# A new order for a projection's seven products, earlier regroups, later deviations, and another queue for the filters, in an FFT-filter and SoLU kernel

The kernel runs on 1 core of one Trainium2 chip. The metric is the device time of one execution in microseconds (us), lower is better. Times are medians; a ratio is the mean time of one kernel's fast runs over the mean of the kernel before's fast runs of the same rounds, so it is not quite the ratio of the two medians.

## The reference

A Fourier filter over the sequence, then an expansion with a softmax-weighted activation and a layer norm, all in fp32 (in short form, not the file's own lines):

```python
X = np.fft.rfft(x, axis=1)                      # x: 8 x 3136 x 256
y = np.fft.irfft(X * (filt_r + 1j * filt_i), n=3136, axis=1)
h = y.reshape(25088, 256) @ w_in                # 256 -> 1024
e = np.exp(h - h.max(-1, keepdims=True))
solu = h * e / (e.sum(-1, keepdims=True) + 1e-9)
ln = (solu - solu.mean(-1)) / np.sqrt(solu.var(-1) + 1e-6) * g_ln
out = ln @ w_out                                # 1024 -> 256
```

## The kernel before

The Fourier part is done as matmuls (pa, pb, the filter multiplication on VectorE, pc, py), entry by entry, beside the expansion of the entries already done. Its last pc matmul starts at 1368 us in this kernel; some py matmuls follow until 1547 us. What comes after is called the pure part: only the two layers are left, and the last four pairs, with no first layer beside them, are the tail.

Tokens are taken in 98 pairs of blocks of 128. Both layers of a pair are done by seven products each (a Strassen-Winograd scheme), which share few banks of PSUM, the memory that TensorE's sums stand in (m0 to m2 for the first layer, o0 and o1 for the second): a product either starts a bank or adds to what stands in it, and between two of them ScalarE or VectorE must take the intermediate sum away. This is called an evacuation, or a hand-over where TensorE waits for it. Here are the second layer's products, called P1 to P7 below; the first layer's are called by number alone.

```python
def project(p, m):
    bank = {1: 0, 6: 0, 5: 0, 3: 0, 2: 1, 7: 1, 4: 1}[m]
    if m in (1, 2):
        pos[p, bank] = ps_o.tile(...)           # one buffer for o0, one for o1
    s1, s2, s3, s4 = solu_sums[p]               # sums of regrouped rows, from GpSimd
    lhs = {1: solu_ts[p, 0][0], 2: solu_ts[p, 0][1], 4: solu_ts[p, 1][1], 5: s1, 6: s2, 7: s3, 3: s4}[m]
    for f in range(KF // 2):
        nc.tensor.matmul(out=pos[p, bank], lhsT=lhs[:, f, :], rhs=w[:, f, :],
                         start=f == 0 and m in (1, 2, 7), ...)
```

The program order is written by hand, one step per block, two steps per pair. The order of the products, with the bar standing for the work on the other engines in the middle of a step:

| | even step | odd step |
|---|---|---|
| before | 1, P5, 2 / 6, P3, P4, 7 | 5 / P1, P2, 3, 4, P6, P7 |
| after | 1, P6, 2 / P5, 6, 7, P3 | P1, P2, 5 / P7, 3, 4, P4 |

Two kinds of transfer matter here, both through SyncE's queue. `regroup` turns the activated rows into the layout that the projection reads, with eight DMAs of 128 KB per pair; it reads the result of the turn, a transposition on VectorE. `regroup_deviations` does it for the layer norm's factors (`rs_t`), with four DMAs of 0.5 KB per two pairs. Every evacuation of a projection multiplies by `rs_t`, so the first one of a pair cannot start without it. The code, cut at the dots:

```python
# even step, before                    # odd step, before
...                                    ...
regroup(j - 3, 0)  # 4 DMAs, then      project_sums(j - 3, 0)
                   # rows <- rs        if (j - 3) % 2 == 0:
...                                        regroup_deviations((j - 3) // 2)   # a pair ahead of use
project(p, 3); project(p, 4)           project(p, 6); project(p, 7)
regroup(j - 3, 1)  # 4 DMAs
```

Of the kernel before, what the change touches and what calls it, by code (L numbers as in the profile page):

```python
# [80 lines left out]
def kernel(  # L81
# [70 lines left out]
    class Spectrum:  # L152
# [72 lines left out]
        def multiply(self, i, parts):  # L225
# [14 lines left out]
            if 1 in parts:  # L240
                turned, pt = self.turned.pop(i), self.prods[i]
                nc.vector.tensor_tensor(out=turned, in0=turned, in1=part(1), op=ALU.mult)  # L242
                nc.vector.tensor_tensor(out=pt, in0=pt, in1=turned, op=ALU.add)
                del self.fs[i]
# [38 lines left out]
    with ExitStack() as st:  # L283
# [93 lines left out]
        for i in range(NS):  # L377
            sp.turn(i)
            sp.multiply(i, (0, 1))
# [40 lines left out]
    def load_filter(s, count):  # L420
        f = fpool.tile([P, 2, 2, C], FP32, name=f"f_{s}", tag="f")
        for p in range(2):
            nc.gpsimd.dma_start(out=f[NQ * p:NQ * p + NQ, 0:count],
                                in_=f_dram[s:s + count].rearrange("s q k c -> q s k c"))
        return f
# [135 lines left out]
    def regroup(p, i):  # L561
# [10 lines left out]
        if not second and i == 0:  # L572
# [4 lines left out]
            rs_rows[g] = rows = rs_dram.tile([P, 4], FP32, name=f"rows_{g}", tag="rows")  # L577
            nc.sync.dma_start(out=rows, in_=rs)
# [23 lines left out]
    def project(p, m):  # L602

        bank = {1: 0, 6: 0, 5: 0, 3: 0, 2: 1, 7: 1, 4: 1}[m]
# [17 lines left out]
    def keep_out(p, i, to):  # L622
        rs = out_half(p, i, 0)[1]
        nc.scalar.activation(out=out_half(p, *to)[0], in_=pos[p, 0], func=AFT.Copy, scale=rs)  # L624

    def finish_out(p, i, n, kept, bank):
        ot, rs = out_half(p, i, n)
        if kept is None:
            nc.vector.tensor_scalar(out=ot, in0=pos[p, bank], scalar1=rs, scalar2=None, op0=ALU.mult)  # L629
        else:  # L630
            nc.vector.scalar_tensor_tensor(out=ot, in0=pos[p, bank], scalar=rs,  # L631
                                           in1=out_half(p, *kept)[0], op0=ALU.mult, op1=ALU.add)

    def store_out(p):
# [13 lines left out]
        [[] for _ in range(blocks + LAG + 1)] for _ in range(8))  # L648
# [17 lines left out]
    for n in range(1, len(GROUPS)):  # L666
# [11 lines left out]
        for i, t in enumerate(spread(len(sp.units), *spectrum_at)):  # L678
# [5 lines left out]
            for part in range(2):  # L684
# [24 lines left out]
    def step(k):  # L709
        j, odd = divmod(k, 2)  # L710
        p = j - (LAG - 1) // 2 if odd else j - (LAG + 1) // 2
        if not 0 <= p < pairs:
            p = None
        hid, proj = k < blocks, p is not None
        if odd and j + 1 < pairs:
            pair_sums(j + 1)
        for job in stores[k] + products[0][k] + first_of[k]:
            job()
        if not odd:
# [3 lines left out]
            if proj:  # L723
                project(p, 5)
                keep_out(p, 1, (0, 1))
            if hid:
                product(j, 2)
        else:
            if hid:
                product(j, 5)  # L730
                keep(j, k - 1, 1)
# [4 lines left out]
        for job in products[1][k]:  # L736
            job()
        if not odd:
            if proj:
                finish_out(p, 1, 1, (0, 1), 1)  # L740
            if hid:
                finish(j, k, 0, (k, 0), 1)
        elif hid:
            finish(j, k, 1, (k - 1, 1), 2)
        if 2 <= k < blocks + 2:
            exponential(k - 2)
        for job in early[k]:
            job()
        if not odd:
            if hid:  # L750
                product(j, 6)
                keep(j, k + 1, 0)
            if proj:
                project(p, 3)
                project(p, 4)
            if 0 <= j - 3 < pairs:
                regroup(j - 3, 1)
            if 0 <= j - 4 < pairs:
                project_sums(j - 4, 1)
            if hid:  # L760
                product(j, 7)
        else:
            if proj:
                project(p, 1)
                keep_out(p, 0, (0, 0))
                project(p, 2)
                finish_out(p, 0, 0, (0, 0), 1)
# [3 lines left out]
            if 0 <= j - 3 < pairs:  # L771
                project_sums(j - 3, 0)
                if (j - 3) % 2 == 0:
                    regroup_deviations((j - 3) // 2)
            if proj:
                project(p, 6)
                project(p, 7)
        if 2 <= k < blocks + 2:
            normalize(k - 2)
        if not odd:  # L780
            if proj:
                finish_out(p, 0, 1, None, 0)
                finish_out(p, 1, 0, (1, 0), 1)
                store_out(p)
        else:
            if hid:
                finish(j, k - 1, 1, None, 0)
                finish(j, k, 0, (k, 0), 2)
            if proj:
                keep_out(p, 1, (1, 0))  # L790
# [39 lines left out]
```

## Time and profile before

| | before |
|---|---|
| median | 1791.24 us (3 runs, 1781.95 to 1801.8); 1786.6 us in the rounds with the changed kernel |
| span of the profiled run, granted clock | 1779.0 us, 0.979 |
| TensorE's bare work (see below) | 1611.8 us |
| gaps between matmuls | 161.3 us: 115 up to 400 us, 33 from 400 to 1700 us, 13 after |

The two last rows are reckoned as the prediction does it: each matmul record is given the distance at which such records follow each other when nothing waits (0.429, 0.216 and 0.112 us for 512, 256 and 128 columns), and whatever the next start lies later is a gap. Busy times can't be used for that, as the ends of pipelined matmuls are modelled. The lines themselves are shown in the prediction.

In profile lines PE is TensorE (PEld its weight loads), DVE VectorE, ACT ScalarE, POOL GpSimd, and SPq SyncE's queue. The lines of kernel.py that matter, before and (in brackets) changed: first layer's products L500 (L502), projection's L612 (L619), filter product pb L210; ScalarE's scaling by `rs_t` L624 (L631), VectorE's L629 (L636) and L631 (L638); the first layer's reductions L521 and L524 (L523 and L526), the normalization between them L548 (L550).

### The profile page before, as it was taken

The page shows a single profiled execution, that of the slowest core. Times are in us where ns is not written, and L with a number is a line of the kernel's source. Part 1 is how long each engine was busy: PE and PEld are TensorE (multiplying, and loading weights), DVE is VectorE, ACT ScalarE, POOL GpSimd, SP SyncE. Part 2 cuts the span into 40 slices and gives each one's busy share as a digit, 9 for nine tenths or more (in the row PEclk, how much of TensorE's full clock was granted, in tenths as well). Part 3 has the DMA queues.
Part 4 walks back from the last instruction along what each step waited for, and adds up shares of the span by engine and source line. Part 5 has one row for each costly group of instructions (what it writes and reads, how often), then busy time and mean ns, then how long its engine had stood idle before and what let it go on. Part 6 is the DMA issues. An engine that isn't in the chain of part 4 may idle for free.

```text
span 1779.0 us, 28627 instructions
## 1 busy us (share of the span) xinstructions
PE 1671.6 (94%) x8692; PEld 1141.3 (64%) x8692; DVE 1244.1 (70%) x2586; ACT 1068.4 (60%) x1917; POOL 1093.9 (61%) x1290
## 2 busy tenths in 40 slices
PE   6688887899999999999999999989999999999996
PEld 1225445676666666766667667767777777777776
DVE  0793654578877875678798766767767777777773
ACT  2365555566767666666667666656666566655551
POOL 3242354677767775667877656546666656676664
PEclk9789998999999999999999999999999999999999
DMA  9876687897788865566777665557776444444443
GB/s 279 259 253 184 207 216 197 245 247 211 201 240 231 223 173 158 135 188 188 195 188 200 156 153 157 139 141 186 192 188 158 113 116 114 120 106 107 104 114 94
DMA packets 358120, 314.57 MB, mean 177 GB/s; under 512 B 60833, under 2 KB 318882, under 8 KB 357968
## 3 DMA queue, kind: packets, MB, share of 16 engines
q1 hardware_dynamic: 295664, 187.23, 41.0%
q0 software_dynamic: 29152, 86.45, 16.3%
q10 hardware_dynamic: 33152, 39.07, 7.7%
q8 instruction: 71, 1.16, 0.3%
q14 instruction: 81, 0.66, 0.1%
HBM read 131.65 MB, written 81.50 MB: 120 GB/s over the span
## 4 chain that ended last, share of the span: by engine, by line
PE 74%; DMA 11%; DVE 6%; ACT 3%; issue 3%; SPq 1%; POOL 1%; ACTq 0%; POOLq 0%; DVEq 0%
PE o L612 28%; PE m L500 28%; PE py L277 6%; PE pa L183 4%; PE pb L210 4%; PE pc L252 3%; DMA t<-d 2%; DMA x<-in_x_dram 2%; DMA d<-t 2%; DVE h L548 1%; DMA solu_t<-turn 1%; DMA f<-f_dram 1%; DMA de<-de_tbl 1%; ACT e L532 1%; DVE i L242 1%
## 5 line engine op out<-in xcount | busy, mean ns | idle before, releaser
L550 ACT ACTIVATE e<-h,nmu 128x1024 f32<-128x1024 f32 x196 | 225.3, 1150 | 307.9 <-DVE h L548 305.7
L612 PE MATMUL o<-w_out_sb,solu_t 128*128 128x128 f32 x3136 | 401.9, 277 | 3.0 <-DVE ot L629 1.9
L612 PEld LDWEIGHTS o<-w_out_sb,solu_t 128*128 128x128 f32 x3136 | 382.1, 193 | 33.6 <-issue 28.5
L500 PE MATMUL m<-w_in_sb,s 128*128 128x512 f32 x784 | 397.3, 598 | 6.3 <-ACT h L510 6.3
L612 PEld LDWEIGHTS o<-w_out_sb,u 128*128 128x128 f32 x2352 | 306.5, 192 | 148.7 <-issue 115.7
L612 PE MATMUL o<-w_out_sb,u 128*128 128x128 f32 x2352 | 312.7, 276 | 9.0 <-ACT ot L624 7.7
L479 POOL TENSOR_TENSOR u<-solu_t 128x512 f32<-128x512 f32 x98 | 153.9, 1571 | 265.8 <-DMA solu_t<-turn 152.3
L500 PE MATMUL m<-w_in_sb,y 128*128 128x512 f32 x588 | 304.5, 601 | 6.3 <-DVE h L521 3.5
L548 DVE SCALAR_TENSOR_TENSOR h<-e,rsum,h 128x1024 f32<-128x1024 f32 x196 | 291.8, 1489 | 7.1 <-DVE rsum L545 0.3
L631 DVE SCALAR_TENSOR_TENSOR ot<-o,rs_t,ot 128x128 f32<-128x128 f32 x294 | 102.5, 349 | 257.3 <-ACT ot L624 216.6
L479 POOL TENSOR_TENSOR u<-solu_t,u 128x512 f32<-128x512 f32 x98 | 144.7, 1477 | 173.1 <-PE o L612 171.6
L558 DVE STREAM_TRANSPOSE turn<-h 128x1024 f32<-128x1024 f32 x196 | 242.2, 1236 | 1.5
L524 DVE CUSTOM_DVE_ANT_0 h<-m,h 128x512 f32<-128x512 f32 x196 | 134.8, 688 | 138.3 <-ACT h L510 89.8
L510 ACT COPY h<-m 128x512 f32<-128x512 f32 x294 | 173.0, 589 | 91.3 <-PE m L500 77.9
L532 ACT ACTIVATE e<-h,nmax 128x1024 f32<-128x1024 f32 x196 | 224.5, 1146 | 0.0
L500 PEld LDWEIGHTS m<-w_in_sb,s 128*128 128x128 f32 x784 | 130.6, 192 | 79.2 <-issue 74.2
L277 PEld LDWEIGHTS py<-wi_t,t 100*128 100x128 f32 x1024 | 133.3, 195 | 62.9 <-issue 39.8
L183 PE MATMUL pa<-x,wf_t 98*100 98x512 f32 x256 | 141.7, 662 | 26.6 <-DMA x<-in_x_dram 20.7
L479 POOL TENSOR_TENSOR solu_t<-solu_t,solu_t 128x512 f32<-128x512 f32 x98 | 157.0, 1602 | 7.7
L277 PE MATMUL py<-wi_t,t 100*128 100x98 f32 x1024 | 134.9, 277 | 15.2 <-DMA t<-d 10.4
L500 PEld LDWEIGHTS m<-w_in_sb,y 128*128 128x128 f32 x588 | 99.3, 192 | 74.2 <-issue 50.8
L280 ACT COPY y<-py 128x392 f32<-128x392 f32 x128 | 108.2, 845 | 56.2 <-PE py L277 54.6
(72 smaller groups left out, 2049.1 us busy)
## 6 DMA issues: line engine op xcount, KB each, us to landing
solu_t<-turn SPq DMA_DIRECT2D x784, 128.0 KB
d<-g POOLq DMA_DIRECT2D x99, 256.0 KB, 5.5
out_dram<-ot SPq DMA_DIRECT2D x196, 128.0 KB
t<-d SPq DMA_DIRECT2D x56, 400.0 KB
d<-t POOLq DMA_DIRECT2D x96, 200.0 KB, 4.8
t<-d ACTq DMA_DIRECT2D x74, 256.0 KB
x<-in_x_dram SPq DMA_DIRECT2D x48, 392.0 KB
f<-f_dram POOLq DMA_DIRECT2D x104, 128.0 KB, 4.2
```

Source lines behind the costliest of these rows:

```text
L183: nc.tensor.matmul(out=ps[0:NK, j], lhsT=wf_t, rhs=self.xs[i][0:NR, 2 * u:2 * u + 2, :], start=True, stop=True)
L277: nc.tensor.matmul(out=psv[:, i, :], lhsT=t4s[e, ch][:, i, cb * P:cb * P + P], rhs=wi_t, start=True, stop=True)
L280: evac(out=y[:, cb, t0:t0 + S].rearrange("p (r n) -> p n r", n=NH)[:, n0:n0 + NCH, :], in_=psv)
L479: nc.gpsimd.tensor_tensor(out=out, in0=in0, in1=in1, op=op)
L500: nc.tensor.matmul(out=ms[j, bank], lhsT=lhsT, rhs=w_in_sb[:, w, :], start=m in (1, 2, 7), stop=True, skip_group_check=True)
L510: nc.scalar.copy(out=h_half(k, i), in_=ms[j, 0])
L524: nc.vector.tensor_tensor_reduce(out=h_half(k, i), in0=ms[j, bank], in1=h_half(*kept), scale=1.0, scalar=sofar, op0=ALU.add, op1=ALU.min, ...
L532: nc.scalar.activation(out=e, in_=hs[k], func=AFT.Exp, bias=nmaxs.pop(k)[:, 1:2], scale=-1.0, accum_out=esum)
L548: nc.vector.scalar_tensor_tensor(out=solu, in0=e, scalar=rsum, in1=solu, op0=ALU.mult, op1=ALU.mult, accum_out=nmu)
L550: nc.scalar.activation(out=e, in_=solu, func=AFT.Square, bias=nmu, scale=-float(DFF), accum_out=variances[g][:, i:i + 1])
L558: nc.vector.transpose(out=turns[g][:, :, i, :], in_=solus.pop(k).rearrange("p (f j) -> p f j", j=32))
L612: nc.tensor.matmul(out=pos[p, bank], lhsT=lhs[:, f, :], rhs=w[:, f, :], start=f == 0 and m in (1, 2, 7), stop=True, skip_group_check=True)
```

## The change

Intent: the products that read the regrouped rows' own tiles (P1, P2, P4, and P7, whose sum GpSimd has written over some of the rows) all come in one step and those that read GpSimd's other sums (P6, P5, P3) in the next; the eight regroups go to the top of the even step, so that the rows arrive earlier; the filters' DMAs leave GpSimd for SyncE. To make it fit, the deviations are stored and regrouped later, and the filter multiplication's last addition is split off. The exponential also moves ahead of the reductions and of product 5's copy.

```diff
             if 1 in parts:
+                turned = self.turned[i]
+                nc.vector.tensor_tensor(out=turned, in0=turned, in1=part(1), op=ALU.mult)
+            if 2 in parts:
                 turned, pt = self.turned.pop(i), self.prods[i]
-                nc.vector.tensor_tensor(out=turned, in0=turned, in1=part(1), op=ALU.mult)
                 nc.vector.tensor_tensor(out=pt, in0=pt, in1=turned, op=ALU.add)
...
-            nc.gpsimd.dma_start(out=f[NQ * p:NQ * p + NQ, 0:count],
+            nc.sync.dma_start(out=f[NQ * p:NQ * p + NQ, 0:count],
...
         if not odd and 0 <= j - 3 < pairs:
             regroup(j - 3, 0)
+            regroup(j - 3, 1)
... (the products move as in the table above, with the evacuations and the exponential)
         if not odd:
...
             if 0 <= j - 4 < pairs:
                 project_sums(j - 4, 1)
+                if (j - 4) % 2 == 0:
+                    regroup_deviations((j - 4) // 2)
         else:
...
                 if (j - 3) % 2 == 0:
-                    regroup_deviations((j - 3) // 2)
+                    store_deviations((j - 3) // 2)
```

More of the change, by code (lines that the diff above doesn't have):

```diff
@@ L378 @@
             sp.turn(i)
-            sp.multiply(i, (0, 1))
+            sp.multiply(i, (0, 1, 2))
             if i + 1 < NS:
@@ L422, in load_filter @@
         for p in range(2):
-            nc.gpsimd.dma_start(out=f[NQ * p:NQ * p + NQ, 0:count],
-                                in_=f_dram[s:s + count].rearrange("s q k c -> q s k c"))
+            nc.sync.dma_start(out=f[NQ * p:NQ * p + NQ, 0:count],
+                              in_=f_dram[s:s + count].rearrange("s q k c -> q s k c"))
         return f
@@ L576, in regroup, with store_deviations @@
             nc.gpsimd.tensor_tensor(out=rs, in0=rs, in1=neg_half, op=ALU.pow)
-            rs_rows[g] = rows = rs_dram.tile([P, 4], FP32, name=f"rows_{g}", tag="rows")
-            nc.sync.dma_start(out=rows, in_=rs)
+            rs_rows[g] = rs
+    def store_deviations(g):
+        rows = rs_dram.tile([P, 4], FP32, name=f"rows_{g}", tag="rows")
+        nc.sync.dma_start(out=rows, in_=rs_rows[g])
+        rs_rows[g] = rows
     def regroup_deviations(g):
@@ L620, in out_half, with keep_out, finish_out @@
         return ots[p][:, i, P * n:P * n + P], rss[p // 2][:, 2 * (p % 2) + i:2 * (p % 2) + i + 1]
-    def keep_out(p, i, to):
-        rs = out_half(p, i, 0)[1]
-        nc.scalar.activation(out=out_half(p, *to)[0], in_=pos[p, 0], func=AFT.Copy, scale=rs)
-    def finish_out(p, i, n, kept, bank):
+    def keep_out(p, i, n, bank):
         ot, rs = out_half(p, i, n)
-        if kept is None:
+        nc.scalar.activation(out=ot, in_=pos[p, bank], func=AFT.Copy, scale=rs)
+    def finish_out(p, i, n, bank):
+        ot, rs = out_half(p, i, n)
+        if (i, n) == (0, 1):
             nc.vector.tensor_scalar(out=ot, in0=pos[p, bank], scalar1=rs, scalar2=None, op0=ALU.mult)
         else:
-            nc.vector.scalar_tensor_tensor(out=ot, in0=pos[p, bank], scalar=rs,
-                                           in1=out_half(p, *kept)[0], op0=ALU.mult, op1=ALU.add)
+            nc.vector.scalar_tensor_tensor(out=ot, in0=pos[p, bank], scalar=rs, in1=ot, op0=ALU.mult,
+                                           op1=ALU.add)
     def store_out(p):
@@ L647 @@
     first_of, early, mid, late, stores, loads, *products = (
-        [[] for _ in range(blocks + LAG + 1)] for _ in range(8))
+        [[] for _ in range(blocks + LAG + 1)] for _ in range(9))
     def spread(count, start, over):
@@ L683 @@
             early[t].append(lambda sp=sp, i=i: sp.turn(i, bufs=1))
-            for part in range(2):
+            for part in range(3):
                 products[part][t + 1].append(lambda sp=sp, i=i, part=part: sp.multiply(i, (part,)))
@@ L711, in step, with run @@
         p = j - (LAG - 1) // 2 if odd else j - (LAG + 1) // 2
-        if not 0 <= p < pairs:
-            p = None
-        hid, proj = k < blocks, p is not None
+        hid, proj = k < blocks, 0 <= p < pairs
+        def run(jobs):
+            for job in jobs:
+                job()
         if odd and j + 1 < pairs:
             pair_sums(j + 1)
-        for job in stores[k] + products[0][k] + first_of[k]:
-            job()
+        run(stores[k] + products[0][k] + first_of[k])
         if not odd:
@@ L723, in step @@
             if proj:
-                project(p, 5)
-                keep_out(p, 1, (0, 1))
+                project(p, 6)
+                keep_out(p, 1, 0, 0)
             if hid:
@@ L728, in step @@
         else:
+            if proj:
+                project(p, 1)
+                keep_out(p, 0, 0, 0)
+                project(p, 2)
             if hid:
                 product(j, 5)
-                keep(j, k - 1, 1)
         if 3 <= k < blocks + 3:
@@ L735, in step @@
             regroup(j - 3, 0)
-        for job in products[1][k]:
-            job()
+            regroup(j - 3, 1)
+        if proj:
+            finish_out(p, *((0, 0) if odd else (1, 0)), 1)
+        run(products[1][k])
+        if 2 <= k < blocks + 2:
+            exponential(k - 2)
+        if hid:
+            if odd:
+                keep(j, k - 1, 1)
+                finish(j, k, 1, (k - 1, 1), 2)
+            else:
+                finish(j, k, 0, (k, 0), 1)
+        run(products[2][k] + early[k])
         if not odd:
             if proj:
-                finish_out(p, 1, 1, (0, 1), 1)
-            if hid:
-                finish(j, k, 0, (k, 0), 1)
-        elif hid:
-            finish(j, k, 1, (k - 1, 1), 2)
-        if 2 <= k < blocks + 2:
-            exponential(k - 2)
-        for job in early[k]:
-            job()
-        if not odd:
+                project(p, 5)
+                finish_out(p, 1, 1, 0)
             if hid:
@@ L752, in step @@
                 keep(j, k + 1, 0)
+                product(j, 7)
             if proj:
                 project(p, 3)
-                project(p, 4)
-            if 0 <= j - 3 < pairs:
-                regroup(j - 3, 1)
             if 0 <= j - 4 < pairs:
                 project_sums(j - 4, 1)
-            if hid:
-                product(j, 7)
+                if (j - 4) % 2 == 0:
+                    regroup_deviations((j - 4) // 2)
         else:
             if proj:
-                project(p, 1)
-                keep_out(p, 0, (0, 0))
-                project(p, 2)
-                finish_out(p, 0, 0, (0, 0), 1)
+                project(p, 7)
+                keep_out(p, 1, 1, 1)
             if hid:
@@ L773, in step @@
                 if (j - 3) % 2 == 0:
-                    regroup_deviations((j - 3) // 2)
+                    store_deviations((j - 3) // 2)
             if proj:
-                project(p, 6)
-                project(p, 7)
+                project(p, 4)
         if 2 <= k < blocks + 2:
@@ L781, in step @@
             if proj:
-                finish_out(p, 0, 1, None, 0)
-                finish_out(p, 1, 0, (1, 0), 1)
+                finish_out(p, 0, 1, 0)
                 store_out(p)
-        else:
-            if hid:
-                finish(j, k - 1, 1, None, 0)
-                finish(j, k, 0, (k, 0), 2)
-            if proj:
-                keep_out(p, 1, (1, 0))
-        for job in mid[k] + late[k] + loads[k]:
-            job()
+        elif hid:
+            finish(j, k - 1, 1, None, 0)
+            finish(j, k, 0, (k, 0), 2)
+        run(mid[k] + late[k] + loads[k])
         if k < 4:
```

## The prediction

> **What bounds the kernel now.** I read the page first (sections 1, 2, 4), then the busy time of each engine in a stretch, then TensorE's timeline, then the waits.
>
> ```profile
> PE 1671.6 (94%) x8692; PEld 1141.3 (64%) x8692; DVE 1244.1 (70%) x2586; ACT 1068.4 (60%) x1917; POOL 1093.9 (61%) x1290
> PE   6688887899999999999999999989999999999996
> PE 74%; DMA 11%; DVE 6%; ACT 3%; issue 3%; SPq 1%; POOL 1%; ACTq 0%; POOLq 0%; DVEq 0%
> 400.00:1700.00 1300.00, 1280.69 (x7076) 911.20 (x7075) 976.78 (x2051) 833.17 (x1519) 875.56 (x1000) 1.00 0.62 164
> ```
>
> TensorE is nearly full from slice 7 on, at the full clock. How full, its timeline late in the run tells (start, busy us, line, count):
>
> ```profile
> 1601.00 1.88 PE L500 MATMUL m<-w_in_sb,s 128*128 128x512 f32 x4
> 1602.72 1.95 PE L612 MATMUL o<-w_out_sb,solu_t 128*128 128x128 f32 x16
> 1604.50 1.02 PE L500 MATMUL m<-w_in_sb,s 128*128 128x512 f32 x2
> ...
> 1611.48 1.05 PE L612 MATMUL o<-w_out_sb,u 128*128 128x128 f32 x8
> 1612.37 1.06 PE L612 MATMUL o<-w_out_sb,solu_t 128*128 128x128 f32 x8
> 1613.26 1.45 PE L500 MATMUL m<-w_in_sb,s 128*128 128x512 f32 x3
> ```
>
> Starts tell more than busy times: 4 passes of 512 columns take 1602.72 - 1601.00 = 1.72 us, 0.43 each; 16 of 128 columns take 1.78 us, 0.112 each. One pair of blocks needs 14 x 0.43 + 56 x 0.112 = 12.3 us, and the same place in the next pair comes 1613.26 - 1601.00 = 12.26 us later: no gap at all. Adding 0.43, 0.216 (256 columns) and 0.112 over all matmul records of 400 to 1700 us gives 1272 us of 1300. So the steady part can give back about 28 us at most, 1.6%; before 400 us lie some 115 us of gaps (loads, stores, ScalarE evacuations of the first phase) that the change hardly touches; after 1700 us some 13.
>
> **What the Trainium skill says.** "PSUM — Partial Sum Buffer", section "PSUM bank collisions raise a hardware error": two engines must not use one bank's quadrant at a time, and software has to guard it. So a product that starts a bank anew waits until the last evacuation of the bank has read it; the trace agrees where two such steps stand next to each other, in the last microseconds:
>
> ```profile
> 1769.44 1.06 PE L612 MATMUL o<-w_out_sb,u 128*128 128x128 f32 x8
> 1770.53 0.37 ACT L624 ACTIVATE ot<-o,rs_t 128x128 f32<-128x128 f32 x1 [1.42 <-PE o L612]
> 1770.93 0.35 DVE L631 SCALAR_TENSOR_TENSOR ot<-o,rs_t,ot 128x128 f32<-128x128 f32 x1 [3.12 <-ACT ot L624]
> 1771.05 1.13 PE L612 MATMUL o<-w_out_sb,u 128*128 128x128 f32 x8 [0.55 <-ACT ot L624]
> ```
>
> The second group should start 8 x 0.112 = 0.90 us after the first, at 1770.34; it starts at 1771.05. One evacuation that nothing hides costs 0.71 us. "SBUF — State Buffer", section "Who interferes with whom": a VectorE instruction with two SBUF inputs and a GpSimd instruction that reads SBUF exclude each other, and the one issued first keeps the port. The trace agrees: L548 takes 1.28 us in two thirds of its runs, up to 2.4 us when a GpSimd sum was under way (mean on the page 1489 ns). "DMA: Bandwidth & Descriptors", section "SWDGE vs HWDGE vs iDMA": descriptors of GpSimd's DMAs are made by software on GpSimd, those of SyncE by hardware. Here two filter DMAs occupy GpSimd's sequencer for 1.2 to 1.3 us, and land 4.2 us after issue (section 6).
>
> **The change part by part.** Call projection's products P1 to P7; P1, P6, P5, P3 fill bank o0 in that order, P2, P7, P4 bank o1. P1 and P2 start their banks, P7 starts o1 again. The counts of matmuls, evacuations and DMAs stay as they are. The matmul floor is unchanged.
>
> (a) *Order of products.* Before, the even step has P5 P3 P4, the odd one P1 P2 P6 P7; after, the odd one P1 P2 P7 P4, the even one P6 P5 P3. Before, between P3 and the next pair's P1 (same bank, evacuated by VectorE's L629) stood P4 and two of the first layer's products, 0.9 + 0.86 + 0.86 = 2.6 us. After, only the jobs of the Fourier part put at the even step's end stand there. The built order of the changed kernel shows 97 such successions; in 44 of them nothing stands between, 40 before the last four pairs. Each must wait: last pass of P3 to VectorE's start 0.31 us (lines [.. <-PE o L612] have this start-to-start distance throughout), L629 0.347, to TensorE's restart 0.14, together 0.80 against 0.11 without a wait: 0.69 us. 40 x 0.69 = 28 us. Where a Fourier product of 0.86 us stands between, it covers the wait. This term is the surest: it lies on TensorE itself, which bounds.
>
> (b) *A shorter way from product 5 to the next pair.* In the odd step VectorE does, in this order: L524 on product 5's kept half, L543, L545, L548, L521; and L521 has to read bank m0 before the next pair's product 1 may start. From product 5's second pass: ScalarE's copy starts after 0.63 and takes 0.59, L524 to L548 0.98 (1215.33 to 1216.31 in the trace), L548 to L521 1.21, L521 to the product 0.81: 4.25 us with the short hand-overs. Before, 4 projections and 2 products follow: 0.43 + 4 x 0.90 + 1.72 = 5.7 us, enough. After, P1 and P2 have moved ahead of product 5: 0.43 + 2 x 0.90 + 1.72 = 3.94 us. It lacks 0.31 us, and when L548 meets a GpSimd sum (u1 or s3 run just there) about 0.4 us more. 31 pairs have no Fourier product in that odd step to cover it: 31 x 0.7 = 22 us.
>
> (c) *rs_t later.* The four DMAs of the deviations move from one pair ahead to the end of the even step, behind eight regroup DMAs (0.62 us each); ScalarE needs them at P1's end. My reckoning: the second four regroups 2.7 + 1.85 + about 2 us of landing = 6.6 to 8 us after the even step starts, needed at 7.9. Some 3 us over the run, more in the tail.
>
> (d) *Filters through SyncE.* This takes 104 + 48 DMA issues, about 0.6 us each, from GpSimd, which is no bound; what counts is that they no longer stand behind GpSimd's waits. The one large gap of the steady part comes from that:
>
> ```profile
> 1175.18 1.37 POOL L479 TENSOR_TENSOR u<-solu_t 128x512 f32<-128x512 f32 x1 [10.35 <-DMA solu_t<-turn]
> ...
> 1177.83 1.31 POOL L423 DMA_DIRECT2D f<-f_dram  x2
> ```
> ```profile
> 1178.27 7.18 issue
> 1185.45 2.05 PE pb L210 x4
> ```
>
> GpSimd stood 10.35 us at a regroup, so the filter was issued late, its multiplication freed pb's single bank late, and TensorE stood 7.2 us. With the smaller waits of pb for that multiplication (2.4 us) I expect 9 us back. The earlier regroups and the other places of the products should remove a further 6 us of small waits (m0 for L521, o1 for L631).
>
> (e) *Tail.* In the last four pairs no first-layer product stands between. Now 0.71 us per pair is bare (P5 to P3); after the change five hand-overs are: P2-P7, P7-P4, P6-P5, P5-P3, P3-P1, 3.5 us per pair, 14 us against the 13 us that the tail loses now, partly to other waits: +3 us.
>
> Sum: 28 + 22 + 3 + 3 - 9 - 6 = +41 us. For a possible gain in the first 400 us, where filters now arrive by the other queue, I take off 4: +37, so 1791 + 37 = 1828 us.
>
> **Rivals.** *The early regroups pay.* GpSimd waits 152 us for them, which looks like a prize:
>
> ```profile
> POOL u L479 <- DMA solu_t<-turn: 152.3, 53, 10.3
> DVE ot L631 <- ACT ot L624: 216.6, 158, 3.2
> PEld o L612 <- ACT ot L624: 27.5, 61, 2.6
> PE o L612 <- ACT ot L624: 7.7, 10, 2.5
> ```
>
> But the last two lines show how little of such waits reaches TensorE: 7.7 us of matmul waits for ScalarE's evacuations, most of them in the tail, and 1.3 us for the sums on GpSimd. If (b) is fully covered and all 28 us of gaps go, the time is about 1791 + 28 - 28 = 1790. *SyncE becomes the bound.* It issues per pair 8 regroups (5 to 7 us), 2 stores (1.3), deviations (1.2) and now up to 4 filter DMAs (2 to 2.4) besides loads: 11 to 13 us of some 16 in the Fourier stretches. It has room, but it is strictly in order, and one late landing pushes all behind it; a wait of SyncE for the turn lasts up to 11.3 us already. If that starves P1 or the multiplications in the middle of the run, 1850 to 1870. *VectorE becomes the bound*: 977 of 1300 us busy, the same work after; its order alone matters, which is (b).
>
> **Range and chances.** Term (a) is nearly certain, so a gain over 2% is all but excluded: even all steady gaps together are 1.6%. (b) may be 8 to 30 us, (d) 0 to 15, the rest 10 either way. Sum +7 to +69 us; the three times of before spread by 20 us themselves. Range 1798 to 1860. The limit of 2% is at 1827, almost at my value, so: faster 0.03, same 0.47, slower 0.50.
>
> **What would show it.** In TensorE's timeline after 1500 us a pair should take 13.3 to 13.7 us instead of 12.3, with a gap of 0.69 us before P1 put down to VectorE's scaling (the line that answers to L629), and one of 0.3 to 1 us before product 1 put down to the line that answers to L521. TensorE's waits for these two should sum to about 50 us, and the 7 us gap at pb should be gone. Wrong it would be if P1 does not wait there, if waits for f, rs_t or the regroup fill the table of waits instead, or if the first 400 us move by more than 10 us.

## The result

The changed kernel takes 1934.43 us (4 runs, 1930.41 to 1941.99) against 1786.6 us (4 runs), a ratio of 1.082, 95% interval 1.0738 to 1.0902. It is slower, to which the prediction gave 0.50 (0.47 to no change), but by 148 us instead of 37, and outside its range.

First the page (busy time of each engine; chain of waits by engine) and the busy time of the middle stretch, in the order span, PE, PEld, DVE, ACT, POOL, clock, DMA share, GB/s.

```profile
PE 1721.1 (89%) x8692; PEld 1158.0 (60%) x8692; DVE 1236.5 (64%) x2586; ACT 1086.1 (56%) x1917; POOL 909.5 (47%) x1138
...
PE 58%; DMA 13%; DVE 12%; ACT 6%; SPq 4%; issue 3%; POOL 2%; ACTq 0%; POOLq 0%; DVEq 0%
```
```profile
400.00:1700.00 1300.00, 1208.61 (x6453) 844.86 (x6453) 883.10 (x1851) 782.72 (x1394) 647.45 (x791) 0.98 0.58 157
```

Before, 7076 matmuls ran in this stretch; now it is 6453. GpSimd has become emptier, as meant (1093.9 to 909.5 us), and no other engine is nearer to full. The chain has moved from PE (74 to 58%) to VectorE (6 to 12%), ScalarE (3 to 6%) and SyncE's queue (1 to 4%). TensorE's bare work is the same 1611.8 us; its gaps have grown from 161.3 to 314.0 us, that is by 152.7 of the span's 153.1 us. Of that, 17 us lie before 400 us, 127 in the middle and 8 in the end (the last 79 us).

Now the pure part, TensorE's timeline (start, busy us, line, count, idle before and what ended it):

```profile
1704.65 1.05 PE L619 MATMUL o<-w_out_sb,u 128*128 128x128 f32 x8
1706.15 2.05 PE L619 MATMUL o<-w_out_sb,solu_t 128*128 128x128 f32 x16 [0.44 <-DVE ot L636]
...
1711.56 1.05 PE L619 MATMUL o<-w_out_sb,solu_t 128*128 128x128 f32 x8
1713.63 1.13 PE L502 MATMUL m<-w_in_sb,y 128*128 128x512 f32 x2 [1.02 <-DVE h L523]
...
1727.62 1.12 PE L502 MATMUL m<-w_in_sb,y 128*128 128x512 f32 x2 [0.70 <-DVE h L523]
```

Line 1 is P3, line 2 the next pair's P1 and P2. P1 should start 0.90 us after P3 and starts 1.50 after it: this is term (a). Line 3 is P4, line 4 product 1 of the next pair, 2.07 us later instead of 0.90: term (b). The pair takes 1727.62 - 1713.63 = 13.99 us; 12.26 before, 13.3 to 13.7 predicted. So far the prediction's mechanism stands. Over the run after 400 us, gaps of this kind before P1 sum to 27.0 us (45 cases) and before product 1 to 27.1 us (37 cases). The idle times in the table below are smaller, because they count from the modelled end of the matmul before.

The rest is in the Fourier part. The table of waits (engine, line, what it waited for: us in all, times, longest):

```profile
ACT ot L631 <- DMA rs_t<-rows: 105.8, 24, 8.3
...
PE o L619 <- POOL u L481: 29.1, 9, 6.4
...
PE m L502 <- DVE h L523: 20.9, 31, 1.0
...
PE o L619 <- DVE ot L636: 19.7, 44, 0.6
```

The first line is new; in the kernel before it was

```profile
ACT ot L624 <- DMA rs_t<-rows: 3.7, 1, 3.7
```

ScalarE now stands up to 8.3 us for the deviations. What that does to TensorE is seen in one place at 440 to 455 us:

```profile
439.35 9.35 SPq L572 DMA_DIRECT2D solu_t<-turn  x8
...
448.80 3.39 SPq L590 DMA_DIRECT2D rs_t<-rows  x4
...
454.03 0.37 ACT L631 ACTIVATE ot<-o,rs_t 128x128 f32<-128x128 f32 x1 [5.80 <-DMA rs_t<-rows]
...
454.43 0.35 DVE L638 SCALAR_TENSOR_TENSOR ot<-o,rs_t,ot 128x128 f32<-128x128 f32 x1 [5.63 <-ACT ot L631]
...
454.88 2.04 PE L619 MATMUL o<-w_out_sb,solu_t 128*128 128x128 f32 x8 [3.86 <-POOL u L481]
```

SyncE is busy with the eight regroups until 448.70: in this stretch the trace puts 3.9 us down to one regroup that waited for the landing of a load (t), and from 441.37 to 445.28 us SyncE issues nothing. Only then come the four small DMAs, of which the third waits 1.5 us for a load too; they are issued until 452.19, and the last lands at about 454.0. ScalarE's scaling of P1 has waited for it since 448.2, VectorE's scaling of P2 for ScalarE's, and P7, which starts P2's bank anew, for VectorE's: 3.86 us. The label of that last wait names GpSimd's sum, but that ended at 453.09 + 1.25 = 454.34; VectorE ended at 454.78, 0.10 us before the matmul. A releaser is inferred from semaphore events; where two come close together, ends of both should be looked up. So the line "PE o <- POOL u" in the table above is probably for a good part this wait.

There are 22 places where ScalarE waits more than 1 us for `rs_t`. Adding up TensorE's gaps from 7 us before to 3.5 us after the ScalarE instruction gives 75.9 us; in the kernel before there is one such place, with 1.3 us.

Not all of these gaps are waits. Between 400 and 1700 us the granted TensorE clock is 0.50 in eight stretches of 3.4 or 6.8 us, 41 us together, each beside a gap of 2.5 us or more (the first from 453.9 us, with the wait above). Inside them a pass of 512 columns takes 0.85 us and one of 128 columns 0.21, about twice the usual. By an estimate from these passes this adds about 17 us to the passes, against 1.6 us in the kernel before and in the order-alone run below, which have one such stretch each. So about 15 of the middle's 127 us are not waiting but slow matmuls after it.

"Perfetto Trace Analysis", section "DMA Instruction — HWDGE (DVE, Sync)" in the Trainium skill, says that the sequencer waits for the DMA's semaphores before it hands it over, and that the profiled time is only the handing over, not the movement of data. The trace agrees: the issue of the four ended at 452.19 and the reader started 1.84 us later. While the sequencer waits, nothing behind it in the program can be issued, however ready it is.

### The profile page after: what moved, and what is told of

Same layout as the page of the kernel before. It is cut to its first block, busy times and chain, and to the rows that moved or that the text cites. A ratio compares the mean times of both kernels' runs of the same rounds, so it can differ in the third digit from the quotient of the medians.

```text
span 1932.1 us, 28147 instructions
## 1 busy us (share of the span) xinstructions
PE 1721.1 (89%) x8692; PEld 1158.0 (60%) x8692; DVE 1236.5 (64%) x2586; ACT 1086.1 (56%) x1917; POOL 909.5 (47%) x1138
## 4 chain that ended last, share of the span: by engine, by line
PE 58%; DMA 13%; DVE 12%; ACT 6%; SPq 4%; issue 3%; POOL 2%; ACTq 0%; POOLq 0%; DVEq 0%
PE o L619 23%; PE m L502 21%; PE py L279 5%; PE pa L183 4%; DVE h L550 4%; PE pc L254 3%; DMA de<-de_tbl 2%; SPq L572 2%; DMA t<-d 2%; DVE h L526 2%; DMA d<-t 2%; PE pb L210 2%; DMA f<-f_dram 2%; DMA rs_t<-rows 2%; DMA x<-in_x_dram 2%
## 5 line engine op out<-in xcount | busy, mean ns | idle before, releaser
L619 PEld LDWEIGHTS o<-w_out_sb,solu_t 128*128 128x128 f32 x3136 | 392.5, 195 | 215.8 <-issue 59.4
L619 PE MATMUL o<-w_out_sb,solu_t 128*128 128x128 f32 x3136 | 417.9, 282 | 100.2 <-POOL u L481 29.1
L502 PE MATMUL m<-w_in_sb,y 128*128 128x512 f32 x588 | 313.0, 616 | 21.4 <-DVE h L523 20.9
L481 POOL TENSOR_TENSOR u<-solu_t,u 128x512 f32<-128x512 f32 x98 | 125.7, 1282 | 356.3 <-PE o L619 356.2
L550 DVE SCALAR_TENSOR_TENSOR h<-e,rsum,h 128x1024 f32<-128x1024 f32 x196 | 281.9, 1438 | 7.1 <-DVE rsum L547 0.3
L631 ACT ACTIVATE ot<-o,rs_t 128x128 f32<-128x128 f32 x294 | 108.1, 368 | 209.8 <-DMA rs_t<-rows 105.8
L262 POOL DMA_DIRECT2D d<-g x101 | 76.4, 756 | 224.1 <-ACT g L257 215.6
L481 POOL TENSOR_TENSOR u<-u,solu_t 128x512 f32<-128x512 f32 x98 | 125.5, 1281 | 113.2 <-PE o L619 111.4
L502 PEld LDWEIGHTS m<-w_in_sb,s 128*128 128x128 f32 x784 | 128.9, 195 | 66.9 <-issue 61.5
```

Source lines behind the costliest of these rows:

```text
L481: nc.gpsimd.tensor_tensor(out=out, in0=in0, in1=in1, op=op)
L502: nc.tensor.matmul(out=ms[j, bank], lhsT=lhsT, rhs=w_in_sb[:, w, :], start=m in (1, 2, 7), stop=True, skip_group_check=True)
L550: nc.vector.scalar_tensor_tensor(out=solu, in0=e, scalar=rsum, in1=solu, op0=ALU.mult, op1=ALU.mult, accum_out=nmu)
L631: nc.scalar.activation(out=ot, in_=pos[p, bank], func=AFT.Copy, scale=rs)
```

## The experiments

I had two theories. "Deviations": `rs_t` is late because it stands behind eight regroups in SyncE's queue. "Filters": the filters' DMAs have made that queue late. Both leave the two hand-overs (a) and (b) as they are. A third question is whether the order of the products costs anything beyond (a) and (b). Each kernel computed the right result.

### One part undone: filters back on GpSimd

```diff
-            nc.sync.dma_start(out=f[NQ * p:NQ * p + NQ, 0:count],
+            nc.gpsimd.dma_start(out=f[NQ * p:NQ * p + NQ, 0:count],
```

> The changed kernel with one part undone: the filters' DMAs go back from SyncE to GpSimd. Theory 'deviations' (rs_t is regrouped at the end of the even step, behind eight regroup DMAs on the in-order SyncE queue, just before it is needed; worth about 70 of the 148 us): the filters are only part of what stands in that queue, so a part of it comes back, 10 to 35 us, 1900 to 1925 us, and ScalarE still waits for rs_t in the Fourier stretches (before the run: 105.8 us in 24 waits), perhaps half of it. Rival 'filters' (it is the filter DMAs that make SyncE late): about 70 us come back, 1865 us, and the waits for rs_t fall under 20 us. The hand-overs (VectorE's scaling before P1, its reduction before product 1) stay at about 54 us on TensorE in both.

Measured: 1924.38 us, ratio 1.074 (1.0706 to 1.0775). Only 10 us come back, the low end of the first theory, and its table of waits still has

```profile
ACT ot L631 <- DMA rs_t<-rows: 74.4, 15, 8.2
```

So the deviations are late without the filters in the queue too.

### The other part undone: deviations a pair early again

```diff
         if not odd and 0 <= j - 3 < pairs:
             regroup(j - 3, 0)
             regroup(j - 3, 1)
+            if (j - 3) % 2 == 0:
+                store_deviations((j - 3) // 2)
...
-                if (j - 4) % 2 == 0:
-                    regroup_deviations((j - 4) // 2)
...
-                    store_deviations((j - 3) // 2)
+                    regroup_deviations((j - 3) // 2)
```

> The changed kernel with one part undone: the deviations are stored right after the even step's regroups and regrouped in the odd step that follows, a pair before their use, as in the kernel before. Filters stay on SyncE. Theory 'deviations': ScalarE's waits for rs_t fall from 105.8 us to under 10, and about 70 us come back: 1855 to 1880 us; what stays over the kernel before is the two hand-overs, about 54 us, plus some 20. Rival 'filters': SyncE is as full as it was, the lateness only shows elsewhere (regrouped rows, filter multiplication): 1905 us or more.

Measured: 1911.69 us, ratio 1.0678 (1.0647 to 1.071). The wait for `rs_t` is gone (1.4 us), but only 23 us come back. That is the rival's answer: something else is late now.

```profile
DVE p L238 <- DMA f<-f_dram: 119.1, 36, 8.5
```

VectorE's filter multiplication waits for its filter, 17.2 us in the changed kernel, 119.1 here. Neither theory alone was right.

### Both undone: the order alone

> The changed kernel with both undone: filters on GpSimd and deviations early. What is left of the change is the order of the products and the regroups at the top of the even step. If the two hand-overs are all that this order costs, it is the kernel before plus about 54 us (27.1 us of waits for the first layer's reduction, 27.0 us for projection's scaling, as counted in the changed kernel's trace): 1840 us. If it comes out above 1870, the order costs something beyond the two hand-overs that I have not found. If below 1815, the hand-overs were partly a consequence of the late deviations.

Measured: 1852.06 us, ratio 1.0342 (1.0319 to 1.0366). With both undone 82 us come back, not 10 + 23. So either of the two, alone, costs most of what both cost: 72 us (deviations, filters on GpSimd), 60 us (filters, deviations early). What is left is 63 us above the kernel before, a little more than the two hand-overs.

### The filters alone, in the kernel before

> The kernel before with one part of the change alone: the filters' DMAs through SyncE. My prediction gave this part -9 us, with the 7 us gap before the filter product at 1178 us gone: 1777 to 1785 us. Rival 'filters': the queue gets late for the regrouped rows and the deviations here too: 1800 us or more.

Measured: 1862.99 us, ratio 1.0409 (1.0386 to 1.0432): 74 us slower, where the prediction had 9 us faster. VectorE waits longer for filters, before and here:

```profile
DVE p L238 <- DMA f<-f_dram: 25.8, 12, 7.7
```
```profile
DVE p L238 <- DMA f<-f_dram: 118.4, 40, 6.2
```

The filter product's gaps on TensorE after 400 us are 42 us (11.1 before); 20 us more of gaps than before lie in the first 400 us. One place, at 397 to 410 us: ahead of the filter's two DMAs stand two regroups, whose issue takes 4.2 us, and the output's two stores; the first is issued at 403.31, the second, after 0.7 us of waiting for the landing of an earlier regroup, at 404.69. By then VectorE is ready for the filter; it stands 5.3 us, until 4.6 us after that issue ended.

The issues alone don't fill SyncE: from 400 to 1300 us they take 468 of 900 us in the kernel before, 502 in this run, 478 in the changed kernel. So my reading is that the order counts: GpSimd reaches a filter's DMA when GpSimd's own earlier work is done; SyncE reaches it when the turn, the regroups, the stores and the loads ahead of it in the program have all had their semaphores.

### Filters on SyncE, half a step earlier

```diff
-            ahead(t, 1).append(lambda sp=sp, i=i: sp.fetch_filter(i))
+            early[t - 1].append(lambda sp=sp, i=i: sp.fetch_filter(i))
```

> The kernel before with the filters on SyncE, as in the run that took 1863.0 us, but issued in the middle of the step, ahead of the output's two stores and of the second regroup, in place of after them at the step's end. Theory 'place in the queue' (the filters were late because they stood behind stores and regroups that wait for the step's last results): VectorE's waits for f (118.4 us) fall under 30 us, the filter product's gaps go, and most of the 74 us come back: 1790 to 1810 us. Rival 'load on the queue' (152 more issues and landings on SyncE, eight outstanding at most, make everything late): 1840 us or more.

Measured: 1845.38 us, ratio 1.0336 (1.029 to 1.0382). Only 18 of the 74 us come back. The theory in this narrow form fell, and the time is one that the rival, load on the queue, had named (1840 us or more). The waits for filters halve (61.5 us), but now the filters push back what stands behind them:

```profile
POOL u L479 <- DMA solu_t<-turn: 334.9, 64, 12.3
```

That was 193.2 us with the filters at the end of the step and 152.3 before. So on this queue a better place for one transfer was a worse one for another. But these waits of GpSimd hardly reach TensorE, which waits 0.9 us for such sums. TensorE's gaps at the filter product are still 34 us of 42, those before product 4 and py have grown from 6 to 17 us, and those of the first 400 us are still 19 us above the kernel before. Whether it is the place or the number of transfers on SyncE that costs the rest, no run separates.

### Deviations ahead of the regroups, in the same step

The changed kernel with filters on GpSimd, and the four small DMAs moved from behind the eight regroups to before them:

```diff
+        if not odd and 0 <= j - 4 < pairs and (j - 4) % 2 == 0:
+            regroup_deviations((j - 4) // 2)
         if not odd and 0 <= j - 3 < pairs:
             regroup(j - 3, 0)
...
-                if (j - 4) % 2 == 0:
-                    regroup_deviations((j - 4) // 2)
```

> The changed kernel with filters on GpSimd (1924.4 us), and the deviations' four regroups moved from the end of the even step to its top, ahead of the eight regroups instead of behind them; the step they are issued in and their store stay as the change has them. Theory 'place in the queue': standing behind eight issues of 0.67 us and the waits of those for the turn and for landings is what made rs_t late; then it lands in time, and the time is that of the run with both parts undone, 1845 to 1860 us, with ScalarE's waits for rs_t (74.4 us) gone. Rival 'distance' (a step instead of a pair ahead is too late wherever it stands in the queue): above 1890 us.

Measured: 1854.98 us, ratio 1.0371 (1.0332 to 1.041), and 10.1 us of waits for `rs_t`. Here the place theory holds: nothing but the order of issues within one step changed, and 69 us came back. Nor did the number of transfers on the queue change.

### The two hand-overs, one at a time

Both on the run with filters on GpSimd and deviations early (1852.06 us). First P3 ahead of product 7:

```diff
                 keep(j, k + 1, 0)
-                product(j, 7)
             if proj:
                 project(p, 3)
+            if hid:
+                product(j, 7)
```

> On the run with filters on GpSimd and deviations early (1852.1 us): projection's P3 moves ahead of the first layer's product 7, so that product 7 (0.86 us) stands between P3 and the next pair's P1. My term (a) says that VectorE's scaling of P3 then hides: TensorE's waits for it (27.0 us in 45 cases) fall to the tail's 3 us, and 24 us come back: 1826 to 1832 us. Rival: VectorE is late for other reasons and the wait only moves to another product: above 1845 us.

Measured: 1826.45 us, ratio 1.0225 (1.0175 to 1.0274), 26 us less (21 by the ratios, which is the fairer measure here, as the two runs come from different chips: 1.0342 - 1.0225 = 0.0117 of 1788 us). TensorE's waits for VectorE's scaling fall from 19.7 to 2.2 us in the table of waits. Then P6 ahead of product 1:

```diff
-            if hid:
-                product(j, 1)
-                keep(j, k, 0)
             if proj:
                 project(p, 6)
                 keep_out(p, 1, 0, 0)
             if hid:
+                product(j, 1)
+                keep(j, k, 0)
                 product(j, 2)
```

> On the same run (1852.1 us): projection's P6 moves ahead of the first layer's product 1 in the even step, which gives the reduction that frees bank m0 0.90 us more. My term (b): TensorE's waits for it (28.9 us in 36 cases, 0.80 us each) fall under 6 us and 23 us come back: 1827 to 1833 us. Rival: the wait is one of VectorE's whole queue and grows along with the cover, or P6 now waits for its sum on GpSimd: above 1845 us.

Measured: 1822.42 us, ratio 1.0212 (1.0158 to 1.0265), 30 us less (23 by the ratios); the waits for the reduction fall from 22.7 to 2.1 us. Both terms are shown, on the chip, with about the sizes that the prediction gave them (28 and 22 us).

### Both hand-overs by another odd step

Odd step 5, P1, P2 / 3, P7, 4, P4, with the copy of product 5 earlier.

> On the same run (1852.1 us): the odd step's order becomes 5, P1, P2, 3, P7, 4, P4, with the copy of product 5 ahead of the exponential. This closes both bare hand-overs at once (product 5 stands between P3 and P1, and P1, P2, 3, P7, 4, P4 between product 5 and the next product 1). If (a) and (b) add up, 50 us come back: 1800 us, within 2% of the kernel before, and the early regroups are then seen by themselves: below 1780 us they are worth something, at 1790 to 1805 us nothing. If above 1820 us, the order costs something else.

Measured: 1834.47 us, ratio 1.027 (1.0229 to 1.0311). A miss: 18 us back instead of 50. The waits for VectorE's scaling are gone (2.0 us), but (b) is not closed: before product 1 there are still gaps of 19 us, of 29 in the order-alone run. Before product 4 there are 8 us of new gaps, put down to VectorE's reduction, and before P4 there are now gaps of 28.7 us (24 times) for ScalarE's scaling of P7, with only product 4 between them. This pointed to a third hand-over, P7 to P4: in the order-alone run, with products 3 and 4 between, it costs 15.0 us in 21 cases after 400 us, all in the Fourier part (leaving out the tail).

### All three closed

P3 ahead of product 7, P6 ahead of product 1, and P4 moved from the end of the odd step to behind P6; filters on GpSimd, deviations early.

```diff
             if proj:
                 project(p, 6)
                 keep_out(p, 1, 0, 0)
+                project(p, 4)
             if hid:
                 product(j, 1)
...
-            if proj:
-                project(p, 4)
```

> On the run with filters on GpSimd and deviations early (1852.1 us), the three hand-overs of the order closed at once: P3 ahead of product 7 (measured alone: -26), P6 ahead of product 1 (-30), and P4 moved from the odd step's end to behind P6, because TensorE stood 15 to 20 us (21 cases of 0.7 us) before P4 for ScalarE's scaling of P7, a third hand-over that my prediction did not have. If these three are all that the order costs, the sum is 1852 - 26 - 30 - 16 = 1780 us, level with the kernel before (1786 us) and nothing is left to explain. If it stays above 1805 us, a cost of the order is still unknown.

Measured: 1774.08 us (6 runs, 1765.79 to 1791.26), ratio 0.9937 (0.9895 to 0.998). With the three hand-overs closed, no net cost of the order is left. (A further small cost that its gains make up for is not excluded.) In TensorE's timeline the same product in two pairs that follow each other:

```profile
1608.61 1.06 PE L619 MATMUL o<-w_out_sb,solu_t 128*128 128x128 f32 x8
...
1620.92 1.06 PE L619 MATMUL o<-w_out_sb,solu_t 128*128 128x128 f32 x8
```

12.31 us a pair, as good as bare. This kernel is the fastest, by 0.6% under the kernel before; that is far below 2%, but its interval lies under 1.

### The same with filters earlier on GpSimd

> The same with the filters' DMAs, on GpSimd, issued in the middle of the step instead of at its end, ahead of GpSimd's sums that wait for regrouped rows (the cause of the 7 us gap at 1178 us in the kernel before). Expected: 5 to 10 us less than the run without it, 1770 to 1778 us, so up to 1% faster than the kernel before; no difference if the early regroups have already taken GpSimd's long waits away.

Measured: 1778.33 us, ratio 0.9951 (0.9918 to 0.9983): no difference to the run above. The filter product's gaps after 400 us are under 2 us in that run already, so there was nothing to win.

### The order closed, the queue as the change has it

> The changed kernel with the three hand-overs closed, but its use of the SyncE queue kept as it is (filters on SyncE, deviations regrouped behind the regroups). With the queue mended and the order kept, 1852.1 us; with both mended, 1774.1 us. If the queue's cost does not depend on the order, it is 1934 - 1852 = 82 us here too, so 1774 + 82 = 1856 us, and the waits for rs_t are still near 100 us. Rival: the bare hand-overs gave SyncE time to catch up, so without them the queue is late more often and costs more: above 1870 us; or the late rs_t was partly a consequence of the odd step's P7 coming so soon after P1: below 1840 us.

Measured: 1868.59 us, ratio 1.0442 (1.0399 to 1.0486), between the two expectations: 94 us above the run with the queue mended, where the sum of parts says 82. ScalarE waits 99.1 us for `rs_t`, and TensorE's gaps around those waits are 76.3 us. So the queue's cost stands by itself; whether the 12 us more are the rival's catching up was not tested.

### Where the third hand-over comes from

The change splits the filter multiplication's addition off, behind product 5's reduction. This undoes only that, on the order-alone run:

```diff
-        run(products[1][k])
+        run(products[1][k] + products[2][k])
...
-        run(products[2][k] + early[k])
+        run(early[k])
```

> On the run with filters on GpSimd and deviations early (1852.1 us): the filter multiplication's last addition goes back to where the kernel before has it, in one piece with the second multiplication, ahead of the exponential and of product 5's reduction. The change had split it off. Theory 'late addition': it frees the turned rows late, ScalarE's next copies wait for it (113.9 us in the two lines of that copy's wait, 33.3 in the kernel before), and behind them the scaling of P7 that P4 waits for (15 us in 21 cases): these P4 waits fall under 4 us and 12 to 15 us come back, 1837 to 1842 us. Rival: P4 waits because the new odd step leaves only products 3 and 4 between P7 and P4, wherever the addition stands: no change, 1848 us or more.

Measured: 1840.79 us (1830.32 to 1849.63), ratio 1.0309 (1.0272 to 1.0346). The two lines are from the tables of waits of the order-alone run and of this one:

```profile
PE o L619 <- ACT ot L631: 19.5, 29, 2.2
```
```profile
PE o L619 <- ACT ot L631: 6.4, 13, 0.8
```

In the Fourier part 0.9 us of the 15.0 before P4 are left. So its cause is the late addition. The way there is probably that it frees the turned rows late, ScalarE's copies of the next ones wait, and the scaling of P7 stands behind them; these copies' waits for VectorE fall from 113.9 to 70.8 us, still twice the 33.3 of the kernel before. The time fell by 11 us, but the runs scatter by 19 and the intervals overlap, so the waits carry this, not the time. The same edit where P4 is covered:

> The fastest kernel so far (three hand-overs closed, 1774.1 us) with the same edit. There P4 no longer waits, so the addition's place should be worth nothing: 1768 to 1780 us. Below 1765 us it frees something else.

Measured: 1785.21 us, ratio 0.9977 (0.995 to 1.0003); the interval overlaps that of the run without the edit (0.9895 to 0.998). Its median is 5 us above the range expected, and the gaps of its profiled run are a little smaller (162 against 171 us, where the 171 are from the slowest of the other's six executions), so no difference is shown.

### The sum

| from | to | us by medians | by ratios (of 1788 us) |
|---|---|---|---|
| kernel before 1786 | order with three hand-overs closed 1774 | -12 | -11 |
| 1774 | hand-overs as the change has them 1852 | +78 | +72 |
| 1852 | filters and deviations on the queue as the change has them 1934 | +82 | +85 |

Of the 78 us (72), (a) is 26 (21), (b) 30 (23), and 22 (28) are the third hand-over, the tail and what the three share.

## Why the prediction was wrong

**(a), P3 to P1:** predicted 28 us, 27.0 us in the trace (45 cases), 26 us by experiment (21 by ratios). Right in mechanism and size. (The lines from which the prediction took 0.71 us show P5 and P3; P3 adds to its bank and does not start it anew, but it waits in the same way.)

**(b), product 5 to product 1:** predicted 22 us, 27.1 us in the trace (37 cases), 30 us by experiment (23 by ratios). Right in mechanism and size, also in its two parts: in 5 of the 35 gaps over 50 ns L550 takes 1.28 to 1.37 us and the gap is 0.28 to 0.38 us (0.31 predicted). In the other 30 L550 takes 1.6 to 2.2 us and the gap is 0.6 to 1.2, on average 0.85. So the larger share of (b) is that L550 is longer there. Of the 53 runs of L550 over 1.4 us all had a GpSimd sum under way when they began or within 0.1 us, of the other 147 only 11.

**(c), rs_t later: the step that failed.** The prediction reckoned "the second four regroups 2.7 + 1.85 + about 2 us of landing = 6.6 to 8 us after the even step starts, needed at 7.9", and took 3 us for it. That sum counts only four of the eight regroups that it names; with all eight its own figures give 2 x 2.7 + 1.85 + 2 = 9.25 us, past the 7.9. In the trace at 440 to 455 us the eight regroups take 9.35 us instead of the 5.4 that eight issues of 0.67 us need, the four small ones 3.39 instead of 1.85, and the landing is at 454.0, 14.7 us after the regroups began; needed at 448.2. Beyond that, the reckoning laid the bare issue times end to end, although the same profile showed waits inside that chain: SyncE's regroups waited 51.7 us for landings of earlier loads in the kernel before. Even the 6.6 to 8 us left no slack for the one operand without which no evacuation of the pair starts. With filters on GpSimd this alone costs 72 us where 3 were predicted; 69 of them come back when the order of the issues alone is changed.

**(d), the filters: -9 us predicted, the wrong sign.** Its first half came true: the 7 us gap at the filter product is gone, and its gaps after 400 us are about 3 us instead of 11.1. The failed reasoning is "what counts is that they no longer stand behind GpSimd's waits": it did not ask behind what they stand then. In the kernel before, the move alone costs 74 us; in the new order with the deviations mended, 60 us. And the gain was to be had without it: the closed order keeps the filters on GpSimd, and its gaps there are under 2 us. The 6 us of small waits came back only in the closed order too: gaps before product 1 and P4 are 5.1 and 1.6 us in the kernel before, 0.4 and 0 there.

**The rival "SyncE becomes the bound"** was named, with the right mechanism ("strictly in order, and one late landing pushes all behind it", "starves P1 or the multiplications"), and 1850 to 1870 us. The size fits that cost alone, 94 us on the closed order, 1869 us, but no working stood behind it, so this is partly luck. What was wrong was to treat it as an alternative to (a) and (b). They lie at different places on TensorE and add up.

**Why (c) and (d) don't add up with each other** the waits show: with the deviations early VectorE waits 119.1 us for filters; in the changed kernel only 17.2, and 105.8 us of ScalarE's waits stand in their place. Both come down the same queue in the same step, filters behind deviations, and my reading is that the stretch in which the pair stands for the first gives the second time to land. No run tests that directly.

**The third hand-over** was not in the prediction: it missed that the split-off addition makes ScalarE late for P7. **The tail** was to cost 3 us and costs 8. **The first 400 us** were to give back 4 and cost 17, beyond the 10 us that the prediction set itself as a limit. The profiled run of the closed order still has 12 of these 17, but the other runs with filters on GpSimd have between 6 us less and 12 us more than the kernel before, so part may be scatter; the cause was not looked for. (The upper end of the prediction's range is 5 us more than its parts give, 28 + 30 - 4 + 10 = 64; this changes nothing.)

## What to carry to other kernels

Before a DMA moves to another engine's queue, write down what stands ahead of it there in program order and when the last of those gets its semaphores; a queue can spend little more than half of its time on issues (502 of 900 us here) and still deliver late. Put the operand that every evacuation needs ahead of the long transfers of its step, because bare issue times are only a lower limit of when it lands: 6.6 to 8 us were reckoned, and 14.7 were seen. When products that share PSUM banks are reordered, list every pair of neighbours on a bank and the work between them: each hand-over that was left bare cost 0.6 to 0.8 us on average here, and putting another product in between took it away at no cost that showed.

## What the Trainium skill lacked or had wrong

- "DMA: Bandwidth & Descriptors", section "Issuing engines are not separate DMA queues", says that issuing from several engines only saves the sequencer time of initiating, "which is usually small relative to the DMA itself". Here the choice of the issuing engine alone was worth 74 us of 1789 (filters moved to SyncE in the kernel before), with SyncE's issues filling 56% of the stretch. The section does not say that the choice also decides what a DMA waits for that it doesn't need: whatever stands ahead of it on that engine (3.9 us behind one landing at 441 us in the changed kernel).
- "Perfetto Trace Analysis", section "DMA Instruction — HWDGE (DVE, Sync)", has the sequencer's wait, which lies outside the profiled window, but not how a whole queue's lateness is read. Here it was read from a group of issues, 9.35 us from the first to the last of eight regroups where 5.4 were needed, beside the 5.80 us that the reader of the queue's next transfer waited.
- No page that I read gives the time of a PSUM hand-over between engines. From the traces: last pass of 128 columns to the start of ScalarE or VectorE 0.31 us, of 512 columns 0.63 us, their end to TensorE's next matmul 0.05 to 0.14 us.
